# A mixture layer behind attention: 256 instead of 512 plain tokens, Strassen passes of 1,024 tokens, and output weights decoded ahead

## The chip, the cores and the metric

One Trainium2 chip, one core of it. The metric is device time in microseconds (us) of one execution, and lower is better. The engines are TensorE (PE, with its weight loads as PEld), VectorE (DVE), ScalarE (ACT), GpSimd (POOL), and SyncE (SP), which issues most DMAs. Each engine runs its instructions in the order in which they were compiled and waits at the first one that is not ready.

## What is computed

Attention with eight heads of 64 (four local heads, four strided ones), then two feed-forward layers, the second of them gated:

```python
x = attention(q, k, v)                    # 4 x 576 = 2304 tokens, 512 wide
h = x @ w_in                              # 512 -> 2048
x = (h - tanh(h)) @ w_out                 # 2048 -> 512
xn = x / sqrt(mean(x * x) + 1e-6) * rms_g
out = (silu(xn @ w_gate) * (xn @ w_val)) @ w_out2   # 512 -> 1536 -> 512
```

## The kernel before

**Precision.** Every operand of TensorE is kept as a high and a low part, and a product is three matmuls (high by high, low by high, high by low). A block product over 512 inputs is thus a group of 12 matmuls.

**First layer.** The 2,304 tokens go in five groups of 512, 512, 256, 512 and 512 (g = 0 to 4). A group runs 16 units f: `ps_h` (12 matmuls), tanh on ACT, two DVE steps and an ACT cast for the high and low part of `g`, then 12 matmuls into the four banks `ps_x`. Attention of the next group runs beside it, so in the last group there is none, and the SBUF room of attention (on the right side) is free for other pools. At the end of the last group `evac_x` copies the four banks to `xe` on ACT and writes them to DRAM (`x2d`) by DMAs that ACT issues itself.

**Second layer.** `R0` = 512 tokens are worked plainly, in 12 steps f: gate product `ps_h<-xn,w`, value product `ps_m<-xn,w` (12 matmuls each, `pe_gv`), silu and multiplication to `p`, and `pe_o`, which adds 12 matmuls `ps_x<-w,p` into four banks. Gate and value have two banks each, so gate f needs the silu of gate f-2 to be done. The other 1,792 tokens are worked in two Strassen passes j of 2 x `HT` = 2 x 448 tokens, each with six pairs of steps and seven products a pair (`ps_pr`, `ps_q`), 12 matmuls of `HT` columns for each of gate and value. Then `ps_o` adds the output products. The operands of the Strassen passes (`xt1` to `xt6`) are made from `x2` (the normalised rows, `prep_s`) by casts on ACT and DVE and by four subtractions `tr` on POOL (`conv`).

**Weights.** The second layer's 36 weight tiles (gate, val and out2 of 12 steps) arrive packed (`raw`, 512 KB). Decoding one takes ACT `ct` and `ca`, DVE `ct`, ACT `w` (high) and DVE `w` (low). `Stream` `st2` does this in the order of `w2_order`, the first `N1` = 18 of them during the last group, the others during the plain steps. `Store` writes the results to DRAM (`store`, `plain`), from where the Strassen passes fetch them (`wt<-w`). The unpacked tiles lie in a pool `wts` of 22 slots, and raw tiles go into the same pool or into slots that the first layer's weights leave.

**What sets the order.** SP runs in written order from the last group on. PE runs in written order in groups 1 to 3 and in the Strassen passes. Elsewhere a list scheduler of the compiler puts the instructions of an engine in a row. Pools decide the waits: a tile can be written when the last reader of its slot is done, and a `ps_h` or `ps_m` bank when ACT or DVE has read it.

Of the kernel before, what the change touches and what calls it, by code (L numbers as in the profile page):

```python
# [7 lines left out]
F32 = mybir.dt.float32  # L8
# [26 lines left out]
def attn_moe_moe_kernel(  # L35
# [39 lines left out]
    NG = len(groups)  # L75
    R0 = 512
    HT = 448
    NJ = (NT - R0) // (2 * HT)
# [78 lines left out]
    class Weight:  # L157
# [51 lines left out]
    class Stream:  # L209
# [12 lines left out]
        def step(self):  # L222
            i, ws = self.i, self.ws
            self.load_to(min(len(ws), i + 1 + min(self.ahead, max(1, self.slots - 2 - i))))
            if i < len(ws):
                ws[i].bits(self.on_act(i))
            if 0 < i <= len(ws):
# [93 lines left out]
    decode = Decode()  # L321
    xt, tmp = {}, [wts, None, None]

    class Store:
# [12 lines left out]
        def to(self, n):  # L337
            while self.n < min(n, len(w2_order)):
                w = w2[w2_order[self.n]]
                p, i = divmod(w.f, 2)  # L340
                t = w.t.bitcast(F32)
                if w.kind == "out2":
# [10 lines left out]
    store = Store()  # L353

    xh = {}
# [510 lines left out]
    xn = {}  # L866
    HALVES = [(0, 512), (512, 2 * HT)]

    def preps():
        yield from prep_s(0, [(0, R0)], bank_m, pbr)  # L870
        x = xt["raw"]
        t = mid.tile([128, 2, 4, 512], F32R, tag="xs", name="xn")
        for c in range(4):
            nc.scalar.copy(out=t[:, 0, c], in_=x[:, c, :R0])
            nc.vector.tensor_tensor(out=t[:, 1, c], in0=x[:, c, :R0], in1=t[:, 0, c].bitcast(F32), op=ALU.subtract)
# [9 lines left out]
    def pe_gv(j, f):  # L885
        r, n = [], R0
        for kd, pool, tag in (("gate", ps_h, "h"), ("val", ps_m, "m")):
# [26 lines left out]
    def evac_o(j):  # L914
        for t in range(R0 // 128):
# [3 lines left out]
            else:  # L919
                nc.vector.tensor_scalar_mul(out=o, in0=oacc[j][t], scalar1=WS)  # L920

    def prep_s(base, parts, bank, room):
        w = parts[-1][1]
# [5 lines left out]
        for h, (a, e) in enumerate(parts):  # L929
            n = e - a  # L930
            acc, sq = (pbx.tile([128, 512], F32, tag=nm, name=nm)[:, :n] for nm in ("acc", "sq"))
            nc.scalar.activation(out=acc, in_=x[:, 0, a:e], func=ACTF.Square)
# [84 lines left out]
    class Stage:  # L1017
# [45 lines left out]
        def run(self, outs, tick):  # L1063
# [33 lines left out]
            tick(4)  # L1097
            outs(3)

# [38 lines left out]
    wks = [Work(groups[1])]  # L1138
    xq, first_units, pg = [], units[:3], None
    del units[:3]  # L1140
# [59 lines left out]
    def unit(g, f, a, e, pe_work=lambda: None, work=lambda: None):  # L1200
# [7 lines left out]
        g_hi(g, f, a, e)  # L1208
        if g == NG - 1 and f >= 1:
            st2.to(N1 * f // (FA - 1))  # L1210
            store.plain(st2.i - 1)
            store.to(st2.i - 6)
# [17 lines left out]
    for g, f, a, e in units:  # L1230
        if g == 0:
            st1.to(2 * (f + 4))
        elif f == 0:
            if g == 1:
                queue0.close()
                order = ctx.enter_context(ExitStack())
                order.enter_context(tc.manual_schedule(engines={mybir.EngineType.PE}))
            if g == NG - 1:
                order.close()
            assert not wks[-1].pe and not wks[-1].st  # L1240
# [3 lines left out]
        if g == NG - 1 and f == 0:  # L1244
            ctx.enter_context(tc.manual_schedule(engines={mybir.EngineType.SP}))
            poolT.close()
            poolR = ExitStack()
            pbx = ctx.enter_context(tc.tile_pool(name="pbx", bufs=1, side="right", reuse_waits="tile"))
            pbr = poolR.enter_context(tc.tile_pool(name="pbr", bufs=1, side="right", reuse_waits="tile"))
            tmp[0] = poolR.enter_context(tc.tile_pool(name="tmr", bufs=1, side="right", reuse_waits="tile"))  # L1250
# [19 lines left out]

        unit(g, f, a, e, pe_work, work)
        if g == NG - 1:
            if f == 2:
# [32 lines left out]
    store.to(len(w2_order))  # L1306
    pairs[0].fetch((0, 1))
    ctx.enter_context(tc.manual_schedule(engines={mybir.EngineType.PE, mybir.EngineType.SP}))

    def second():  # L1310
        nonlocal pb, osum
        pe_o(0, FB - 1)
        osum = mid.tile([128, 4096], F32, tag="xs", name="osum").rearrange("p (t n) -> p t n", t=8)
        evac_o(0)
# [6 lines left out]
    for j in range(NJ):  # L1321
        for p in range(NP):
# [34 lines left out]
            st.run(outs, tick)  # L1357
            todo += [(st, t) for t in ((4, 5, 6, 3, 0, 1, 2) if end else range(7))]
    for o, t in todo:
# [98 lines left out]
```

## Time and profile before

| | |
|---|---|
| median of 3 runs | 885.1 us (884.06 to 887.2) |
| the profiled execution | 881.58 us, of which 879.8 us is the span |
| PE busy | 866.9 us, 99% of the span |
| DVE, ACT, POOL busy | 619.3, 407.9, 266.3 us |
| chain that ended last | PE 62%, DVE 9%, POOL 7%, issue 2%, ACT 1% |

The profiled execution is 3.5 us below the median. Its stages: groups 0 to 3 end at about 369 us, the last group's output matmuls at 460.75 us, the plain steps at about 557 us, the first Strassen pass at about 707 us, the second at 876 us. A timeline row gives the start, the time from the first start to the last end, the engine, line, operation and tiles, and the number of instructions in the row. Matmuls overlap by a fraction of one, so the pace is read from the start of one row to the start of the next.

### The profile page before, as it was taken

Reading aid. Unit: us, or ns where it says so; the run is one execution under the profiler, and the core shown is the slowest. Engines: PE = TensorE matmul, PEld = TensorE weight load, DVE = VectorE, ACT = ScalarE, POOL = GpSimd, SP = SyncE. Lnnn points to the kernel's source line nnn. Section 1 sums busy time; section 2 is a strip of 40 time slices with the busy share of each in tenths; the row PEclk is TensorE's granted clock in tenths of the full one; section 3 lists DMA queues with packets and bytes.
Section 4 is the critical chain, followed back from the end, with each engine's and each line's share of the span. In section 5 each row is a group of like instructions: output and inputs, shape, how many; then the busy total and the mean of one; then the engine's idle time right before and its main releaser. Section 6 shows DMA issues by size and latency. Waiting matters only on the chain.

```text
span 879.8 us, 14013 instructions
## 1 busy us (share of the span) xinstructions
PE 866.9 (99%) x5091; PEld 739.5 (84%) x5091; DVE 619.3 (70%) x1273; ACT 407.9 (46%) x914; POOL 266.3 (30%) x317
## 2 busy tenths in 40 slices
PE   6999999999999999999999999999999999999998
PEld 4888888888998887888888888988888888888886
DVE  6999788888689887168958981345977953345444
ACT  7987543233544333287838751345332533422320
POOL 0000247694276952000002375395621300000000
PEclk8999999999999999999999999999999999999999
DMA  9964224311313000189928895698666039955002
GB/s 331 385 205 164 86 78 137 112 50 37 117 54 111 27 17 1 37 310 382 383 78 263 276 360 195 236 411 320 239 232 230 19 131 351 390 173 164 1 0 84
DMA packets 62021, 157.83 MB, mean 179 GB/s; under 512 B 9920, under 2 KB 21056, under 8 KB 61952
## 3 DMA queue, kind: packets, MB, share of 16 engines
q1 hardware_dynamic: 60800, 155.89, 49.9%
q10 hardware_dynamic: 1152, 1.05, 0.4%
q8 instruction: 40, 0.66, 0.3%
q14 instruction: 29, 0.24, 0.1%
HBM read 112.87 MB, written 44.04 MB: 178 GB/s over the span
## 4 chain that ended last, share of the span: by engine, by line
PE 62%; DVE 9%; POOL 7%; issue 2%; ACT 1%; DVEq 0%; ACTq 0%; POOLq 0%
PE ps_pr L150 19%; PE ps_o L150 13%; PE ps_x L150 12%; PE ps_h L150 11%; POOL pr L636 5%; DVE so L676 4%; PE ps_m L150 4%; PE ps_q L150 3%; POOL pr L669 1%; DVE tg L821 1%; DVE g L832 1%; DVE sm L412 0%; DVE x L966 0%; DVE sc L641 0%; ACT sm L423 0%
## 5 line engine op out<-in xcount | busy, mean ns | idle before, releaser
L150 PE MATMUL ps_x<-g,w 128*128 128x512 f32 (+1 forms) x984 | 214.7, 366 | 0.0
L150 PE MATMUL ps_h<-xs,w 128*128 128x512 f32 (+1 forms) x984 | 213.7, 365 | 0.6 <-DVE tg L821 0.6
L150 PEld LDWEIGHTS ps_h<-xs,w 128*128 128x128 f32 x984 | 168.9, 189 | 30.7 <-DVE tg L821 1.0
L150 PEld LDWEIGHTS ps_x<-g,w 128*128 128x128 f32 x984 | 168.5, 189 | 30.2 <-ACT g L827 0.2
L150 PE MATMUL ps_pr<-xt,wt 128*128 128x448 f32 x576 | 122.5, 365 | 0.0
L636 POOL TENSOR_TENSOR pr<-sk,sq 128x256 f32<-128x256 f32 (+2 forms) x101 | 82.7, 855 | 130.0 <-DMA sq<-in_q_str_dram 104.2
L150 PE MATMUL ps_o<-wt,p 128*128 128x512 f32 x504 | 120.2, 390 | 0.0
L150 PEld LDWEIGHTS ps_pr<-xt,wt 128*128 128x128 f32 x576 | 107.9, 188 | 10.3 <-DVE s L1040 0.2
L150 PEld LDWEIGHTS ps_o<-wt,p 128*128 128x128 f32 x504 | 94.6, 188 | 18.7
L827 ACT CAST g<-tg 128x512 fp32r<-128x512 f32 (+1 forms) x82 | 46.5, 567 | 102.1 <-DVE tg L821 101.9
L669 POOL TENSOR_TENSOR pr<-sv,se 128x288 f32<-128x288 f32 (+12 forms) x104 | 69.7, 691 | 56.5 <-DVE so L676 19.8
L1059 ACT COPY u<-ps_pr 128x448 f32<-128x448 f32 x72 | 38.2, 533 | 90.4 <-PE ps_pr L150 90.4
L676 DVE TENSOR_REDUCE so<-pr 128x16 f32<-128x272 f32 (+11 forms) x104 | 65.0, 654 | 8.4 <-POOL pr L669 8.0
L821 DVE SCALAR_TENSOR_TENSOR tg<-ps_h,tg 128x512 f32<-128x512 f32 (+1 forms) x82 | 50.8, 620 | 28.0 <-ACT tg L816 27.9
L816 ACT ACTIVATE tg<-ps_h 128x512 f32<-128x512 f32 (+1 forms) x82 | 44.3, 540 | 48.2 <-PE ps_h L150 48.1
L1110 DVE SCALAR_TENSOR_TENSOR osum<-ps_o,osum 128x512 f32<-128x512 f32 x70 | 48.0, 687 | 23.1 <-PE ps_o L150 22.5
L832 DVE TENSOR_TENSOR g<-tg,g 128x512 fp32r<-128x512 f32 (+1 forms) x82 | 55.4, 677 | 12.3 <-ACT g L827 11.7
L980 POOL TENSOR_TENSOR tr<-x 128x896 f32<-128x896 f32 x4 | 10.3, 2575 | 174.0 <-DVE x L966 174.0
L150 PE MATMUL ps_pr<-xt,wo 128*128 128x448 f32 x288 | 60.7, 365 | 0.4 <-ACT u L1059 0.4
L150 PEld LDWEIGHTS ps_pr<-xt,wo 128*128 128x128 f32 x288 | 54.0, 188 | 5.3 <-ACT u L1059 0.8
L188 DVE SCALAR_TENSOR_TENSOR ct<-ca,ct 128x512 uint32<-128x512 uint32 x68 | 51.1, 763 | 6.2 <-ACT ca L178 4.6
L199 DVE TENSOR_TENSOR w<-ct,w 128x512 fp32r<-128x512 f32 x68 | 49.8, 741 | 5.4 <-ACT w L195 5.1
(114 smaller groups left out, 1130.9 us busy)
## 6 DMA issues: line engine op xcount, KB each, us to landing
wt<-w SPq DMA_DIRECT2D x84, 512.0 KB, 6.3
raw<-in_w_out_dram SPq DMA_DIRECT2D x28, 512.0 KB, 7.3
w<-w SPq DMA_DIRECT2D x24, 512.0 KB, 5.9
w<-wo SPq DMA_DIRECT2D x24, 512.0 KB, 7.3
raw<-in_w_in_dram SPq DMA_DIRECT2D x16, 512.0 KB, 9.2
raw<-in_w_gate_dram SPq DMA_DIRECT2D x12, 512.0 KB, 6.4
raw<-in_w_val_dram SPq DMA_DIRECT2D x12, 512.0 KB, 6.7
v<-ct SPq DMA_DIRECT2D x24, 256.0 KB, 5.6
```

What stands on the lines that cost most here:

```text
L150: nc.tensor.matmul(out_, lhsT, rhs, start=start, stop=stop, skip_group_check=True)
L188: nc.vector.scalar_tensor_tensor(out=t, in0=self.a.bitcast(U32), scalar=3, in1=t, op0=ALU.logical_shift_left, op1=ALU.bitwise_or)
L199: eng.tensor_tensor(out=t[:, 1], in0=self.b, in1=t[:, 0].bitcast(F32), op=ALU.subtract)
L636: nc.gpsimd.tensor_tensor(out=pr, in0=self.k[:, a:e, :], in1=self.q[:, c - c0:c - c0 + 1, :].to_broadcast([128, e - a, D]), op=ALU.mult,)
L669: nc.gpsimd.tensor_tensor(out=pr, in0=self.v[:, 0:c + 1, a:e], in1=self.e[:, c - c0, 0:c + 1].unsqueeze(2).to_broadcast([128, c + 1, e - a ...
L676: pend.append(lambda: nc.vector.tensor_reduce(out=o[:, c - g0, a:e], in_=pr.rearrange("l c d -> l d c"), axis=AX.X, op=ALU.add))
L816: nc.scalar.activation(out=t, in_=h_of[g, f, a], func=ACTF.Tanh, scale=WS)
L821: nc.vector.scalar_tensor_tensor(out=t, in0=h_of.pop((g, f, a)), scalar=WS, in1=t, op0=ALU.mult, op1=ALU.subtract)
L827: nc.scalar.copy(out=t[:, 0], in_=t_of[g, f, a])
L832: nc.vector.tensor_tensor(out=t[:, 1], in0=t_of.pop((g, f, a)), in1=t[:, 0].bitcast(F32), op=ALU.subtract)
L1059: nc.scalar.copy(out=u, in_=x[kd])
L1110: nc.vector.scalar_tensor_tensor(out=o, in0=ps, scalar=WS, in1=o, op0=ALU.mult, op1=ALU.add)
```

## The change

- `R0` goes from 512 to 256 and `HT` from 448 to 512. A plain gate or value group is 12 matmuls of 256 columns, `pe_o` has 6 matmuls of 512 columns and two banks, and a Strassen product has 512 columns. Each pass has eight output tiles of 128 tokens in place of seven.
- A class `Early` decodes all 12 out2 tiles in the last two units of group 3 and the first two of group 4, with three raw slots and three work slots in the room that attention leaves, and stores them to DRAM. `load` fetches them back as finished tiles (`w<-w0_7` and so on) when their plain step is near.
- `st2` therefore decodes gate and val alone, from unit 2 of the last group instead of 1, and `N1` is 19.
- In the plain steps raw tiles have three slots of their own (`rawb`) and wait for no slot of `wts`. `wts` has 20 slots instead of 22 (`HELD` 12).
- The first two Strassen tiles (`wt`) are fetched from step 8 on, and not behind all stores.
- SP's written order begins at unit 14 of group 3.

```diff
-    R0 = 512
-    HT = 448
+    R0 = 256
+    HT = 512
...
-    HELD = 10
+    HELD = 12
...
         def load(self):
             kind, f = self.kind, self.f
-            pool, tag = room_of(w1_at.get((kind, f), 0))
+            if kind == "out2" and f < NE:
+                p, i = divmod(f, 2)
+                self.t = wts.tile([128, 2, 4, 128], F32R, tag="w", name="w")
+                nc.sync.dma_start(out=self.t.bitcast(F32).rearrange("p s c f -> p (s c f)"), in_=pairs[p].store[7 + i])
+                return
+            self.fetch(*(tmp[3] or room_of(w1_at.get((kind, f), 0))))
...
-    N1 = 18
+    N1 = 19
+    NE = 12
...
+    class Early:
...
+        def run(self):
+            ws, n = self.ws, NE
+            for k in range(min(3, n)):
+                ws[k].fetch(self.pool, "r")
+            yield
+            for k in range(n + 2):
+                if k < n:
+                    ws[k].bits(True)
+                    if k + 3 < n:
+                        ws[k + 3].fetch(self.pool, "r")
+                if 1 <= k <= n:
+                    ws[k - 1].split(self.pool, "e", nc.vector)
+                if k >= 2:
+                    p, i = divmod(ws[k - 2].f, 2)
+                    nc.sync.dma_start(
+                        out=pairs[p].store[7 + i], in_=ws[k - 2].t.bitcast(F32).rearrange("p s c f -> p (s c f)")
+                    )
+                yield
...
+        if g == NG - 2 and f == 14:
...
+            ctx.enter_context(tc.manual_schedule(engines={mybir.EngineType.SP}))
...
+            early = Early(soon).run()
...
+    tmp[3] = (poolB.enter_context(tc.tile_pool(name="rawb", bufs=3, reuse_waits="tile")), "raw")
...
     for f in range(FB):
+        if f == FB - 4:
+            pairs[0].fetch((0, 1))
...
-    pairs[0].fetch((0, 1))
```

Three places where instructions stand in another order. First ACT at the end of the last group and the start of the plain steps: `xe` is the copy of a `ps_x` bank, `acc<-ps_r` the first step behind the matmuls of the norm, `xt` an operand for the Strassen passes, `ct`, `ca` and `w` are decoding, and `s` is silu. Before, from the first `xe`:

```order
L852 ACTIVATE xe_5551<-ps_x_4833 128x512
L852 ACTIVATE xe_5555<-ps_x_4834 128x512
L858 DMA x2d_100<-xe_5551 128x256 x2
L858 DMA x2d_100<-xe_5555 128x256 x2
L852 ACTIVATE xe_5559<-ps_x_4835 128x512
L896 ACT_TABLE_LOAD
L896 ACTIVATE s_5617<-ps_h_5604 128x512
L999 CAST xt1_5577<-x2_5114 128x896
```

Of the changed kernel, from the last `xe`. Ahead of these rows stand three `xe`, five of the DMA issues, one `w` cast and the sixth DMA issue:

```order
L890 ACTIVATE xe_5669<-ps_x_4971 128x512
L995 ACTIVATE acc_5530<-ps_r_5642,cole_59 128x512
L1043 CAST xt1_5683<-x2_5238 128x1024
L1043 CAST xt2_5684<-x2_5238 128x1024
L896 DMA x2d_100<-xe_5669 128x256 x2
L203 CAST w_5703<-ct_5606 128x512
L184 ACTIVATE ct_5751<-raw_5597,colf_58 128x512
L186 ACTIVATE ca_5753<-raw_5597 128x512
L184 ACTIVATE ct_5758<-raw_5604,colf_58 128x512
L186 ACTIVATE ca_5760<-raw_5604 128x512
L934 ACT_TABLE_LOAD
L934 ACTIVATE s_5720<-ps_h_5707 128x256
```

The first silu stood behind three `xe`, four DMA issues and the table load, and now stands behind all of the `xe`, all eight DMA issues, the norm's `acc`, both `xt` casts, two `w` casts and the scaling of two raw tiles.

PE at the same place. Before, from the last bank of the last group:

```order
L150 MATMUL ps_x_4836<-g_5486,w_1637 128x512 x3
L150 MATMUL ps_m_5619<-xn_5062,w_4828 128x512 x12
L150 MATMUL ps_h_5669<-xn_5062,w_4932 128x512 x8
L150 MATMUL ps_m_5684<-xn_5062,w_4984 128x512 x12
L150 MATMUL ps_h_5731<-xn_5062,w_5044 128x512 x12
L150 MATMUL ps_m_5746<-xn_5062,w_5094 128x512 x12
```

Of the changed kernel (`ps_h_5707`, gate step 0, has been worked earlier, as `ps_h_5604` before):

```order
L150 MATMUL ps_x_4971<-g_5595,w_1637 128x512 x3
L150 MATMUL ps_m_5722<-xn_5180,w_5016 128x256 x5
L150 MATMUL ps_r_5642<-s2_5576,ones_4923 128x512
L150 MATMUL ps_m_5722<-xn_5180,w_5016 128x256 x3
L150 MATMUL ps_r_5642<-s2_5576,ones_4923 128x512
L150 MATMUL ps_m_5722<-xn_5180,w_5016 128x256 x4
L150 MATMUL ps_h_5769<-xn_5180,w_5070 128x256
L150 MATMUL ps_m_5784<-xn_5180,w_5117 128x256 x12
L150 MATMUL ps_h_5821<-xn_5180,w_5212 128x256 x12
```

The norm's `ps_r` moved from ahead of the last bank into the first value group, and holds a bank of `ps_m` there. `ps_m_5784` takes the bank that `ps_r_5642` leaves when `acc_5530` has read it, and `ps_h_5821` takes the bank that `s_5720` reads.

PE at the end of the plain steps. Before, from the last gate group:

```order
L150 MATMUL ps_h_6316<-xn_5062,w_6153 128x512 x12
L150 MATMUL ps_m_6331<-xn_5062,w_6208 128x512 x12
L150 MATMUL ps_x_5773<-w_6007,p_6246 128x512 x3
L150 MATMUL ps_x_5774<-w_6007,p_6246 128x512 x3
L150 MATMUL ps_x_5775<-w_6007,p_6246 128x512 x3
L150 MATMUL ps_x_5776<-w_6007,p_6246 128x512 x3
```

Of the changed kernel, from the end of output step 10 on:

```order
L150 MATMUL ps_x_5864<-w_6091,p_6292 128x512 x2
L150 MATMUL ps_pr_6356<-xt1_5683,wt_6153 128x512 x6
L150 MATMUL ps_pr_6363<-xt1_5683,wt_6155 128x512 x6
L150 MATMUL ps_m_6322<-xn_5180,w_6215 128x256 x12
L150 MATMUL ps_x_5863<-w_6164,p_6336 128x512 x3
L150 MATMUL ps_x_5864<-w_6164,p_6336 128x512 x3
```

The last value group stood ahead of two output steps and of the first Strassen product, and now stands behind all of these, with its own output step straight behind it.

## Rows read from the trace of the kernel before

**Rows 1.** The page: busy time and share of each engine.

```profile
PE 866.9 (99%) x5091; PEld 739.5 (84%) x5091; DVE 619.3 (70%) x1273; ACT 407.9 (46%) x914; POOL 266.3 (30%) x317
```

**Rows 2.** PE's waits, 340 to 880 us: total, times, longest in us.

```profile
PE ps_pr L150 <- ACT u L1059: 0.4, 1, 0.4
```

**Rows 3.** PE timeline: start, us, operation, tiles, count; 256 and 448 columns.

```profile
232.02 1.60 PE L150 MATMUL ps_x<-g,w 128*128 128x256 f32 x12
233.46 1.60 PE L150 MATMUL ps_h<-xs,w 128*128 128x256 f32 x12
...
706.70 2.59 PE L150 MATMUL ps_pr<-xt,wt 128*128 128x448 f32 x12
709.13 2.59 PE L150 MATMUL ps_q<-xt,wt 128*128 128x448 f32 x12
```

**Rows 4.** PE timeline at the start of the plain steps.

```profile
460.75 2.88 PE L150 MATMUL ps_m<-xn,w 128*128 128x512 f32 x12
...
465.28 2.88 PE L150 MATMUL ps_m<-xn,w 128*128 128x512 f32 x12
468.00 2.88 PE L150 MATMUL ps_h<-xn,w 128*128 128x512 f32 x12
```

**Rows 5.** ACT timeline at the same place (ACTq: issues of DMAs).

```profile
458.90 1.28 ACT L852 ACTIVATE xe<-ps_x 128x512 f32<-128x512 f32 x2
459.65 1.82 ACTq L858 DMA_DIRECT2D x2d<-xe  x4
461.51 0.60 ACT L852 ACTIVATE xe<-ps_x 128x512 f32<-128x512 f32 x1 [1.33 <-DMA x2d<-xe]
462.13 1.28 ACT L896 ACT_TABLE_LOAD   x1
463.42 0.60 ACT L896 ACTIVATE s<-ps_h 128x512 f32<-128x512 f32 x1
...
463.91 0.93 ACT L999 CAST xt<-x 128x896 fp32r<-128x896 f32 x1
...
468.28 0.76 ACT L176 ACTIVATE ct<-raw,colf 128x512 uint32<-128x512 uint16 x1 [0.94 <-DMA x2d<-xe]
468.95 0.66 ACT L178 ACTIVATE ca<-raw 128x512 f32<-128x512 f32 x1
```

**Rows 6.** Costliest groups by form: the 256-column tanh, multiply and cast of group 2.

```profile
L821 DVE SCALAR_TENSOR_TENSOR tg<-ps_h,tg 128x256 f32<-128x256 f32 x20 | 8.4, 418 | 3.1 <-ACT tg L816 3.1
L827 ACT CAST g<-tg 128x256 fp32r<-128x256 f32 x20 | 8.1, 406 | 13.2 <-DVE tg L821 13.2
L816 ACT ACTIVATE tg<-ps_h 128x256 f32<-128x256 f32 x20 | 7.6, 381 | 10.5 <-PE ps_h L150 10.5
```

**Rows 7.** Windows of 2 us at the start: busy of each engine, granted clock, DMA share, GB/s.

```profile
8.00:10.00 2.00, 0.00 (x0) 0.00 (x0) 1.61 (x7) 1.37 (x9) 0.00 (x0) 1.00 1.02 398
...
14.00:16.00 2.00, 2.00 (x34) 1.71 (x32) 1.86 (x9) 2.00 (x10) 0.00 (x0) 0.50 0.98 266
...
18.00:20.00 2.00, 1.33 (x68) 1.02 (x67) 1.86 (x9) 1.75 (x10) 0.00 (x0) 0.98 0.99 395
```

**Rows 8.** PE, DVE and ACT timelines at the last value group and output steps.

```profile
546.88 5.60 PE L150 MATMUL ps_x<-w,p 128*128 128x512 f32 x24
547.15 0.69 DVE L897 SCALAR_TENSOR_TENSOR s<-ps_m,s 128x512 f32<-128x512 f32 x1 [6.09 <-PE ps_m L150]
547.87 0.62 ACT L899 CAST p<-s 128x512 fp32r<-128x512 f32 x1 [2.86 <-DVE s L897]
```

**Rows 9.** POOL and DVE timelines while POOL makes the Strassen operands.

```profile
481.53 2.35 POOL L980 TENSOR_TENSOR tr<-x,tr 128x896 f32<-128x896 f32 x1 [0.65 <-DVE x L966]
481.82 2.61 DVE L188 SCALAR_TENSOR_TENSOR ct<-ca,ct 128x512 uint32<-128x512 uint32 x1
```

**Rows 10.** The page: DMA issues, KB each, median us to landing.

```profile
wt<-w SPq DMA_DIRECT2D x84, 512.0 KB, 6.3
```

**Rows 11.** The window from group 3's end to the first units of group 4.

```profile
340.00:390.00 50.00, 50.00 (x248) 41.26 (x248) 19.74 (x35) 23.28 (x43) 0.00 (x0) 1.00 0.35 117
```

More of the change, by code (lines that the diff above doesn't have):

```diff
@@ L162, in load, with fetch @@
             kind, f = self.kind, self.f
-            pool, tag = room_of(w1_at.get((kind, f), 0))
+            if kind == "out2" and f < NE:
[4 more added lines that the diff above has]
+            self.fetch(*(tmp[3] or room_of(w1_at.get((kind, f), 0))))
+        def fetch(self, pool, tag):
+            kind, f = self.kind, self.f
             r = pool.tile([128, 4, 128], w_in.dtype, tag=tag, name="raw")
@@ L224, in step @@
             self.load_to(min(len(ws), i + 1 + min(self.ahead, max(1, self.slots - 2 - i))))
-            if i < len(ws):
+            if i < len(ws) and not (ws[i].kind == "out2" and ws[i].f < NE):
                 ws[i].bits(self.on_act(i))
-            if 0 < i <= len(ws):
+            if 0 < i <= len(ws) and not (ws[i - 1].kind == "out2" and ws[i - 1].f < NE):
                 pool, tag, eng = self.place(i - 1)
@@ L341, in to @@
                 t = w.t.bitcast(F32)
+                if w.kind == "out2" and w.f < NE:
+                    self.n += 1
+                    continue
                 if w.kind == "out2":
@@ L353, in attn_moe_moe_kernel, with __init__ @@
     store = Store()
+    class Early:
+        def __init__(self, pool):
+            self.pool = pool
+            self.ws = [w2["out2", f] for f in range(NE)]
+        def run(self):
[16 more added lines that the diff above has]
+                yield
     xh = {}
@@ L866, in attn_moe_moe_kernel @@
     xn = {}
[L867 removed]
+    HALVES = [(0, HT), (HT, 2 * HT)]
     def preps():
@@ L930, in prep_s @@
             n = e - a
-            acc, sq = (pbx.tile([128, 512], F32, tag=nm, name=nm)[:, :n] for nm in ("acc", "sq"))
+            if pbs:
+                acc, sq = (pbs.tile([128, 512], F32, tag=nm, name=nm)[:, :n] for nm in ("acc", "sq"))
+            else:
+                t = wts.tile([128, 2, 512], F32, tag="w", name="acc")
+                acc, sq = t[:, 0, :n], t[:, 1, :n]
             nc.scalar.activation(out=acc, in_=x[:, 0, a:e], func=ACTF.Square)
@@ L1097, in run @@
             tick(4)
-            outs(3)
+            outs(3 if HT < 512 else 4)
         def out(self, t):
@@ L1138, in attn_moe_moe_kernel @@
     wks = [Work(groups[1])]
-    xq, first_units, pg = [], units[:3], None
+    xq, first_units, pg, early = [], units[:3], None, None
     del units[:3]
@@ L1208, in unit @@
         g_hi(g, f, a, e)
-        if g == NG - 1 and f >= 1:
-            st2.to(N1 * f // (FA - 1))
+        if g == NG - 1 and f >= 2:
+            st2.to(N1 * (f - 1) // (FA - 2))
             store.plain(st2.i - 1)
@@ L1239, in attn_moe_moe_kernel @@
                 order.close()
-            assert not wks[-1].pe and not wks[-1].st
+            if g < NG - 1:
+                assert not wks[-1].pe and not wks[-1].st
             new_x(g + 1)
@@ L1243, in attn_moe_moe_kernel @@
                 wks.append(Work(groups[g + 1], EARLY if g == 1 else ()))
-        if g == NG - 1 and f == 0:
+        if g == NG - 2 and f == 14:
+            assert not wks[-1].pe and not wks[-1].st
+            order.close()
             ctx.enter_context(tc.manual_schedule(engines={mybir.EngineType.SP}))
+            order = ctx.enter_context(ExitStack())
+            order.enter_context(tc.manual_schedule(engines={mybir.EngineType.PE}))
             poolT.close()
+            poolE = ExitStack()
+            soon = poolE.enter_context(tc.tile_pool(name="soon", bufs=3, side="right", reuse_waits="tile"))
+            tmp[2] = poolE.enter_context(tc.tile_pool(name="ct2", bufs=2, side="right", reuse_waits="tile"))
+            early = Early(soon).run()
+        if g == NG - 1 and f == 2:
+            for _ in early:
+                pass
+            poolE.close()
             poolR = ExitStack()
             pbx = ctx.enter_context(tc.tile_pool(name="pbx", bufs=1, side="right", reuse_waits="tile"))
+            poolS = ExitStack()
+            pbs = poolS.enter_context(tc.tile_pool(name="pbs", bufs=1, side="right", reuse_waits="tile"))
             pbr = poolR.enter_context(tc.tile_pool(name="pbr", bufs=1, side="right", reuse_waits="tile"))
@@ L1271, in attn_moe_moe_kernel @@
         unit(g, f, a, e, pe_work, work)
+        if early is not None and (g < NG - 1 or f < 2):
+            for _ in range(4):
+                next(early, None)
         if g == NG - 1:
@@ L1357, in attn_moe_moe_kernel @@
             st.run(outs, tick)
-            todo += [(st, t) for t in ((4, 5, 6, 3, 0, 1, 2) if end else range(7))]
+            todo += [(st, t) for t in ((4, 5, 6, 7, 3, 0, 1, 2) if end else range(8))]
     for o, t in todo:
```

17 lines of the change are left out of this document (10 added, 7 removed).

## The prediction

> **What bounds the kernel now.** I read the page's busy shares first: PE is busy 866.9 of the 879.8 us of the span, DVE and ACT far less [rows 1]. Then PE's waits: from 340 us to the end there is one, of 0.4 us [rows 2]. So nearly every microsecond from the last groups on is matmul time. Two things can change the end: how many columns PE streams at which pace, and whether the new order puts a wait in front of PE where there was none. Other engines count only where PE reads what they make or needs a bank that they empty. The timelines at the two ends of the plain steps show how much room PE has there [rows 4, 5, 8]. The sum is made against the profiled execution (881.58 us, 3.5 below the median of 885.1), and its difference is then put on the median, since both kernels are timed in ordinary runs.
>
> **Matmuls.** A row's pace is the distance to the next start. Twelve matmuls of 512 columns take 468.00 - 465.28 = 2.72 us [rows 4], 12 of 448 take 709.13 - 706.70 = 2.43, and 12 of 256 take 233.46 - 232.02 = 1.44 [rows 3]. The plain steps have 24 gate and value groups, which become shorter by 2.72 - 1.44 = 1.28 us: -30.7. The Strassen passes have 2 x 6 x 7 products of 12 matmuls, each longer by 0.29: +24.4. Output matmuls move from plain to Strassen, 648 of 512 columns before and after: nothing. The norm's columns follow the tokens: nothing. PE term **-6.3 us**. The 0.29 is a small difference of two rows, and 0.03 more in it would be +2.5, so I keep -6.3 to -3.8.
>
> The Trainium skill (TensorE: Matmul & The Clock Gate, section "Wait — 56ns, not 53.3ns?") speaks against the change here: it gives a warm matmul as its columns at 2.4 GHz plus about 2.5 ns, by which 64 more columns cost 26.7 ns. The rows show 226.7 - 202.5 = 24.2 ns. By the page the PE term would be -30.7 + 26.9 = -3.8 us, an estimate; by the rows it is -6.3.
>
> **The start of the plain steps.** E is the end of the last group's last output matmul, 460.75 us before [rows 4]. Before, silu of gate 0 ran from 463.42 to 464.02, E + 3.3 [rows 5], and gate 2, which needs its bank, started at 468.00 without a wait [rows 4]. Now this silu stands far back in ACT's row. I add up ACT's row with the durations of [rows 5]. A successor starts about 0.1 us before its forerunner ends (463.42 + 0.60 against 463.91), so an operation of 0.60 costs 0.5. The third `xe` can start when its bank is done, about E - 0.2. From E - 0.1 on five DMA issues at 1.82 / 4 = 0.455 take until E + 2.2. The `w` cast waits for the first value group, whose 12 matmuls of 256 columns and two of the norm (1.44 + 0.45) end at E + 1.9, so it runs to about E + 2.7, and a sixth issue beside it. The last `xe` (which also waits for the first copies to reach DRAM, 1.33 us before [rows 5]) and the `acc` behind it end at about **E + 3.9**. PE wants to start `ps_m_5784` at E + 2.0 and needs the bank that `acc` reads: a wait of **1.9 us**. Then come two `xt` casts, 0.93 at 896 columns, so about 0.96 each at 1,024 after the overlap (E + 5.8); a `w` cast (E + 6.3); `ct`, `ca` twice at 0.67 and 0.56 (E + 8.8); the table load, 1.28 (E + 10.0); and silu at 256 columns, 0.38 by the tanh of that width [rows 6]: **E + 10.4**. `ps_m_5784` is through by E + 5.4 at the pace of [rows 3], and `ps_h_5821` needs the bank that this silu reads: a wait of **5.0 us**. Everything behind it on PE is queued. Together **+6.9 us**. The row has 12 to 14 instructions with durations known to a tenth, so I keep +5.5 to +8.5. That nothing hides it is seen from [rows 2]: PE had no idle time here before that the wait could use up.
>
> **PE's clock.** In the trace of before the only comparable idle stretch is near the start: PE does nothing from 8 to 10 us, and then all three windows from 12 to 18 us show a granted clock of 0.50, the lower level of 1.2 GHz, until it is back at 0.98 in 18 to 20 [rows 7]. Six us at half clock are 3.0 us of lost work. In the changed kernel PE works 1.5 of the 8.4 us from E + 2.0 to E + 10.4, so I expect the fall. How much of the low stretch lies beside work and not inside the wait is not shown. Bounds 0 and +3.0; nearer to the row than to nothing, so **+2.0**.
>
> **The end of the plain steps.** Before, the last value group ended at about 546.9, multiplication began at 547.15 and the high cast of `p` ended at 548.49, while PE worked 24 matmuls of older steps [rows 8]. Now `ps_x<-w,p_6336` follows its value group directly. The chain at 256 columns is 0.27 to the start of the DVE step, 0.42, and 0.41 for the cast [rows 6, 8]: **+1.2 us**, between 0.9 and 1.7 (the low part).
>
> The first Strassen product moves ahead of that value group, and its tiles `wt` are fetched earlier. On SP this fetch stands behind the store of a decoded value tile whose ACT work is behind `xt4`, which waits for POOL's fourth `tr`. By the same kind of addition POOL is done at E + 37 to 41, the store is issued at E + 42 to 46, and the tiles land at E + 48 to 53 with 6.3 us a load [rows 10]. PE reaches the product at E + 45.8 by pace alone, and at E + 52.7 or later with the waits above. So the early waits pay for this one: 0 to +2, taken as **+0.6**. The spread of POOL is contention: a DVE decode step of 0.68 us took 2.61 beside a `tr` of 2.35 [rows 9], and `tr` grows by 1024/896. The same stretching could delay a `p` of steps 3 to 5 by up to 4 us without the first wait; behind it this is hidden.
>
> **The last group and the room of attention.** Twelve decodes of three ACT and two DVE steps (about 1.75 and 1.2 us each, 21 and 14 in all, by the paces above) move to 342 to 392 us, where DVE was busy 19.7 and ACT 23.3 of 50 us [rows 11], and out of the plain steps. Both fit, ACT with little to spare. They delay the first loads of gate and value tiles, which stand behind `Early`'s last store on SP. Decode, norm and `xn` then still come some us ahead of PE by my addition, with the tightest places at the last output steps of group 3 and steps 3 and 10 of group 4: 0 to +2, **+0.6**. The Strassen stages give ACT and DVE 512 columns in place of 448 on engines with half their time free: nothing.
>
> **Sum.** -6.3 + 6.9 + 2.0 + 1.2 + 0.6 + 0.6 = **+5.0 us**: 886.6 on the profiled scale, **890.1** on the median's.
>
> **Rivals.**
> (a) Both waits at the start, but the clock stays: for it speaks that the wait is broken by a group of 1.5 us, against it [rows 7]. Without the 2.0 it is +3.0, **888.1**.
> (b) The waits at the start don't arise, and the change is **faster**. The price is ACT's row between the last group's copies and the first silu. It decides from E + 5.4: a silu done by then lets PE through, and then only the end and the last group cost, -6.3 + 1.2 + 0.6 + 0.6 = -3.9, **881.2**. For it speaks that ACT is busy under half of the span [rows 1]; against it, that the row is fixed and ACT cannot take the silu first.
> (c) More is lost in decoding than I count: the moved decodes don't lighten the plain steps, because the loads for gate and value come late and SP's stores hold the Strassen tiles back. It decides where the `wt` tiles land after E + 55. With 2 us in the last group and 4 at the end instead of 1.2 in all, it is +9.8, **894.9**. For it: [rows 9]; against it: the time that the first wait gives.
> (d) By the page's pace for matmuls, everything else as forecast, it is +7.5, **892.6**; [rows 3, 4] speak against it.
>
> **Chances.** Forecast 0.42, (a) 0.20, (b) 0.13, (c) 0.15, (d) 0.10. A measurement of this kernel can tell about 0.3%, 2.65 us, from no change. Case (b) is faster, with some of it within the bound: 0.12. Of (a) about half, and of the forecast a tenth or so where the waits are at their short end, are within: 0.2. The rest is slower: 0.68. The range holds (a), the forecast, (d) and most of (c), and at its low end the forecast with the shortest waits and no fall of the clock (-6.3 + 5.5 + 0.9 = +0.1), and a little of (b): 883.5 to 896.0.
>
> **What would show it.** In the profile of the changed kernel: 12 Strassen matmuls at 2.72 a row; a wait of PE on ACT `acc` of about 1.9 us and one on ACT `s` of about 5 us right behind the last group; ACT's table load some 9 us after E; a granted clock below 1 in the slices behind; a gap of about 1.2 us ahead of the last plain output step. The prediction is wrong if PE waits less than 3 us there, if the product pace is not 2.72, or if PE waits several us in group 4 or at the `wt` tiles.

## The result and the profile after

| | before | after |
|---|---|---|
| median of 6 runs each | 885.37 us (884.06 to 887.81) | 892.89 us (891.12 to 895.17) |
| ratio after : before | | 1.008, 95% interval 1.0059 to 1.0101 |
| the profiled execution, and its span | 881.58, 879.8 | 893.28, 891.5 |

The change makes the kernel 0.8% slower, 7.5 us by the medians. The two profiled executions lie 11.7 us apart in span. Some 2.2 us of that have come up by 26 us, in code that is the same in both (the `ps_v` matmuls that start at 24.07 us before start at 26.29 after), so about 9.5 us are to be explained in these two executions.

The busy shares, which answer to [rows 1]:

```profile
PE 866.0 (97%) x5091; PEld 723.4 (81%) x5091; DVE 633.5 (71%) x1282; ACT 413.3 (46%) x915; POOL 271.0 (30%) x317
```

PE is busy for 0.9 us less, but its share fell from 99% to 97%. PE's waits from 335 us to the end (total, times, longest, in us), which answer to [rows 2]:

```profile
PE ps_h L150 <- ACT s L934: 4.8, 1, 4.8
PE ps_x L150 <- DVE p L938: 2.3, 1, 2.3
PE ps_m L150 <- ACT acc L995: 1.7, 1, 1.7
PE ps_x L150 <- ACT p L937: 1.0, 1, 1.0
PE ps_h L150 <- DVE tg L859: 0.7, 1, 0.7
PE ps_pr L150 <- DVE s L1084: 0.5, 1, 0.5
PE ps_pr L150 <- DVE v L1096: 0.5, 1, 0.5
PE ps_pr L150 <- DVE s L1093: 0.5, 1, 0.5
PE ps_x L150 <- ACT g L865: 0.2, 1, 0.2
```

One wait of 0.4 us has become nine of 12.2 us in all. The one on DVE `tg`, which ends at 335.72 us, is not new: before, it took 0.61 us and ended at 333.50, ahead of the stretch of [rows 2]. PE's timeline at the start of the plain steps, which answers to [rows 4]; E is now 461.84 us:

```profile
463.73 0.28 PE L150 MATMUL ps_h<-xn,w 128*128 128x256 f32 x1
465.67 1.69 PE L150 MATMUL ps_m<-xn,w 128*128 128x256 f32 x12 [1.67 <-ACT acc L995]
472.20 4.98 PE L150 MATMUL ps_h<-xn,w 128*128 128x256 f32 x24 [4.84 <-ACT s L934]
477.02 1.24 PE L150 MATMUL ps_m<-xn,w 128*128 128x256 f32 x9
```

ACT's timeline there, which answers to [rows 5]:

```profile
464.94 0.68 ACT L995 ACTIVATE acc<-ps_r,cole 128x512 f32<-128x512 f32 x1
...
465.51 1.05 ACT L1043 CAST xt<-x 128x1024 fp32r<-128x1024 f32 x1
...
470.47 1.28 ACT L934 ACT_TABLE_LOAD   x1
471.77 0.66 ACT L934 ACTIVATE s<-ps_h 128x256 f32<-128x256 f32 x2
```

`acc` ends at 465.62, E + 3.8. The first silu starts 1.30 us behind the start of the table load and ends at about 472.15, E + 10.3. Both PE waits end where ACT's row says.

Windows of the same stretch (length, busy of PE, PEld, DVE, ACT, POOL with counts, granted clock, DMA share, GB/s):

```profile
470.00:473.00 3.00, 0.80 (x3) 0.80 (x4) 2.91 (x6) 2.97 (x6) 0.00 (x0) 0.50 0.63 179
473.00:480.00 7.00, 7.00 (x42) 6.74 (x42) 6.09 (x13) 4.74 (x10) 0.00 (x0) 0.76 0.94 294
480.00:490.00 10.00, 10.00 (x74) 9.48 (x74) 9.75 (x10) 5.94 (x11) 6.39 (x3) 1.00 0.89 355
490.00:500.00 10.00, 7.67 (x40) 6.77 (x39) 10.00 (x13) 6.15 (x12) 4.03 (x2) 0.83 0.66 186
```

The clock is at its lower level of 1.2 GHz after the long wait, and falls a second time after 490 us. In both places DVE is busy nearly all the time. The second place in the timelines of POOL, DVE and PE, which answers to [rows 9]:

```profile
486.40 2.43 POOL L1024 TENSOR_TENSOR tr<-x,tr 128x1024 f32<-128x1024 f32 x1 [0.77 <-PE ps_m L150]
488.76 2.86 POOL L1024 TENSOR_TENSOR tr<-x 128x1024 f32<-128x1024 f32 x1
...
486.77 2.60 DVE L196 SCALAR_TENSOR_TENSOR ct<-ca,ct 128x512 uint32<-128x512 uint32 x1
489.30 3.41 DVE L1044 TENSOR_TENSOR xt<-x,xt 128x1024 fp32r<-128x1024 f32 x1
...
492.97 0.41 DVE L938 TENSOR_TENSOR p<-s,p 128x256 fp32r<-128x256 f32 x1
493.30 0.68 DVE L196 SCALAR_TENSOR_TENSOR ct<-ca,ct 128x512 uint32<-128x512 uint32 x1
493.90 1.21 DVE L1044 TENSOR_TENSOR xt<-tr,xt 128x1024 fp32r<-128x1024 f32 x1
...
493.43 1.20 PE L150 MATMUL ps_x<-w,p 128*128 128x512 f32 x2 [2.33 <-DVE p L938]
494.43 2.34 PE L150 MATMUL ps_h<-xn,w 128*128 128x256 f32 x10
```

`ct` and `xt` take 0.68 and 1.21 us when POOL is idle (the last two DVE rows). Here each ends 0.54 and 1.09 us after the POOL subtraction that it started beside (489.37 against 488.83, and 492.71 against 491.62), so each spends nearly all of POOL's time waiting. `p`, which PE needs, is queued behind both.

Last, the end of the plain steps, which answers to [rows 3, 8]:

```profile
526.01 1.67 PE L150 MATMUL ps_x<-w,p 128*128 128x512 f32 x6 [0.95 <-ACT p L937]
527.52 2.90 PE L150 MATMUL ps_pr<-xt,wo 128*128 128x512 f32 x12
530.26 2.88 PE L150 MATMUL ps_q<-xt,wt 128*128 128x512 f32 x12
```

### The profile page after: what moved, and what is told of

Same layout as the page of the kernel before. It is cut to its first block, busy times and chain, and to the rows that moved or that the text cites. A ratio compares the mean times of both kernels' runs of the same rounds, so it can differ in the third digit from the quotient of the medians.

```text
span 891.5 us, 14064 instructions
## 1 busy us (share of the span) xinstructions
PE 866.0 (97%) x5091; PEld 723.4 (81%) x5091; DVE 633.5 (71%) x1282; ACT 413.3 (46%) x915; POOL 271.0 (30%) x317
## 4 chain that ended last, share of the span: by engine, by line
PE 58%; DVE 10%; POOL 7%; issue 2%; ACT 2%; DMA 2%; SPq 0%; DVEq 0%; ACTq 0%; POOLq 0%
PE ps_pr L150 20%; PE ps_o L150 14%; PE ps_x L150 9%; PE ps_h L150 9%; POOL pr L674 5%; DVE so L714 4%; PE ps_q L150 4%; PE ps_m L150 1%; POOL pr L707 1%; DVE tg L859 1%; DVE g L870 1%; DMA w<-w 1%; DMA wt<-w 1%; POOL ws L302 0%; DVE sm L450 0%
## 5 line engine op out<-in xcount | busy, mean ns | idle before, releaser
L150 PE MATMUL ps_pr<-xt,wt 128*128 128x512 f32 x576 | 137.4, 390 | 1.5 <-DVE s L1084 0.5
L150 PE MATMUL ps_o<-wt,p 128*128 128x512 f32 x576 | 135.9, 389 | 0.0
L150 PEld LDWEIGHTS ps_o<-wt,p 128*128 128x128 f32 x576 | 108.1, 188 | 22.5
L1103 ACT COPY u<-ps_pr 128x512 f32<-128x512 f32 x72 | 41.9, 587 | 102.4 <-PE ps_pr L150 102.4
L1154 DVE SCALAR_TENSOR_TENSOR osum<-ps_o,osum 128x512 f32<-128x512 f32 x80 | 54.6, 687 | 26.5 <-PE ps_o L150 26.2
L150 PE MATMUL ps_pr<-xt,wo 128*128 128x512 f32 x288 | 67.4, 389 | 0.0
L1024 POOL TENSOR_TENSOR tr<-x 128x1024 f32<-128x1024 f32 x4 | 11.8, 2948 | 176.1 <-DMA raw<-in_w_val_dram 140.8
L870 DVE TENSOR_TENSOR g<-tg,g 128x512 fp32r<-128x512 f32 (+1 forms) x82 | 54.9, 671 | 10.4 <-ACT g L865 9.8
L196 DVE SCALAR_TENSOR_TENSOR ct<-ca,ct 128x512 uint32<-128x512 uint32 x68 | 49.1, 731 | 18.6 <-ACT ca L186 18.1
```

The costliest lines, as they stand in the source:

```text
L150: nc.tensor.matmul(out_, lhsT, rhs, start=start, stop=stop, skip_group_check=True)
L196: nc.vector.scalar_tensor_tensor(out=t, in0=self.a.bitcast(U32), scalar=3, in1=t, op0=ALU.logical_shift_left, op1=ALU.bitwise_or)
L870: nc.vector.tensor_tensor(out=t[:, 1], in0=t_of.pop((g, f, a)), in1=t[:, 0].bitcast(F32), op=ALU.subtract)
L1103: nc.scalar.copy(out=u, in_=x[kd])
L1154: nc.vector.scalar_tensor_tensor(out=o, in0=ps, scalar=WS, in1=o, op0=ALU.mult, op1=ALU.add)
```

## The experiments

Each is a change of the kernel after, or of the experiment that is named. Ratios are to the kernel before, timed beside it on the same chip; since the experiments ran on several chips, ratios compare them better than medians do. "Stretch" is the time from E to the first `ps_pr<-xt,wo`: 65.68 us in the profile after, 96.73 before.

### The order at the start

The pool `pb` of the silu results was opened behind `rawb` and, so I held, lay over room of `xe`. **e1_pb_first** opens it first:

```diff
+    pb = poolB.enter_context(tc.tile_pool(name="pb", bufs=2, reuse_waits="tile"))
     tmp[3] = (poolB.enter_context(tc.tile_pool(name="rawb", bufs=3, reuse_waits="tile")), "raw")
-    pb = poolB.enter_context(tc.tile_pool(name="pb", bufs=2, reuse_waits="tile"))
```

> The changed kernel with two pools in another order: pb (silu and p tiles) is opened ahead of rawb. Theory: silu stands late on ACT only because pb, behind rawb, lies over the room of the xe tiles, whose copies to DRAM must be done first. With pb ahead, the first silu follows the last xe directly and ends at about E + 4.9 (E: end of the last group's output matmuls). PE then waits about 2.9 us instead of 6.9 right behind E, and the clock falls less: 885.5 to 888.5 us, against 892.9 of the changed kernel. Rival (the decode work behind is the limit): PE's wait moves to the p tiles or weights of the later steps, and the time stays above 891.

**e2_pb_first_sp_copies** is e1 with the `x2d` copies of the last group issued by SP:

```diff
-        queue = nc.sync if g < NG - 1 else nc.scalar
+        queue = nc.sync
```

> As the one with pb ahead, and the eight copies of xe to DRAM are issued by SP in place of ACT. Theory: the first silu ends at about E + 2.2, PE waits under 0.5 us there and its clock stays at full speed: 8 to 9 us less than the changed kernel if nothing is given back, 884 to 885; the matmul term alone would be 885.4 - 6.5 = 878.9, and the wait at the p tiles beside POOL's subtractions (2.5 and 1.6 of the clock), the last plain output step (1.1) and the first Strassen pair (1.5) lie on top. Rival: with PE some 7 us earlier the p tiles and Strassen weight tiles come too late by as much, 888 to 892.

e1 took 894.52 us, ratio 1.0118 (1.0084 to 1.0152). Silu came straight behind the last `xe` and the table load, the wait for it was 2.8 us, and none on `acc` was left. e2 took 892.51, ratio 1.0087 (1.0061 to 1.0114), with no wait at the start of the plain steps and the clock at 1.00 there. PE's waits of e2, the largest:

```profile
PE ps_x L150 <- DVE p L938: 3.6, 2, 2.1
PE ps_x L150 <- ACT p L937: 2.1, 3, 1.0
PE ps_pr L150 <- DVE s L1093: 1.2, 2, 0.7
PE ps_m L150 <- ACT w L203: 1.1, 1, 1.1
```

So the order of two pools is what put silu behind the copies, and the wait for it can be removed. But the time stays: the 6.5 us of waits are replaced by others further on, and the clock falls at 505 us instead (0.69 in 505 to 510). The stretch is 63.36 us, 2.3 shorter than after, in a total time that the intervals can't tell from that of the kernel after. What sets the end of the plain steps lies behind PE's first waits.

**e3_filled_wait** puts 40 matmuls of 256 columns, whose result nobody reads, into the first wait, to hold the clock.

```diff
+        if f == 1:
+            fill = bank_x("ps_f")
+            for i in range(40):
+                mm(fill[:, :256], ones, xn[0][:, 0, 0], i == 0, i == 39)
```

> The changed kernel with 40 matmuls of 256 columns (4.8 us, result unused) between gate step 1 and value step 1, where PE waits 6.9 us; silu of step 0 stands one cast later, about 0.5 us. Theory: the wait as a whole stays (2 to 2.6 us of it empty), but the granted clock stays at 1.00 from 463 to 480 us, and the 1.9 us that PE lost at half clock behind the wait come back: 890.5 to 892. Rival (the fall of the clock costs nothing, since the work behind waits for other engines anyway): 893 to 894.

895.8 us, ratio 1.0121 (1.0095 to 1.0147). The clock held at 1.00 from 463 to 470 us, but 3.0 us of the wait for silu were left behind the added matmuls, the clock fell then (0.83 in 470 to 480), and a new wait of 3.0 us on DVE `s` came. It is inconclusive on the clock's price.

### What holds the plain steps

**e4_no_pool** leaves out the four POOL subtractions of the first pass (the operands are made from one summand):

```diff
+            if len(plainly) < 4:
+                plainly.append(name)
+                xt[name] = p
+                return p
```

> The changed kernel with the four subtractions of POOL for the first Strassen pass left out (the casts read one operand as it is); one more cast stands ahead of the first silu, about 1 us. Theory: the wait of 2.3 us of PE for the low part of p of step 3 comes from DVE steps stretched beside POOL, so it vanishes, with the second fall of the clock (1.6 us): 889 to 891. Rival (DVE has too much of its own to do there): the wait stays above 1.5 us and the time is 893 to 894.5.

**e5_no_pool_pb_first** does so on top of e2.

> pb ahead of rawb, copies issued by SP, and the four subtractions of POOL for the first Strassen pass left out (the casts read one operand as it is). Theory: with the wait behind E gone, the plain steps take what DVE needs beside POOL (DVE is busy 10 of 10 us from 480 to 510 in both kernels with pb first, and its steps are stretched); without POOL the stretch from E to the first product with wo falls from 63.4 us to 52.5 to 55 (matmuls alone 51.4), and the time to 881.5 to 885. Rival (DVE's own steps or the loads are the limit): the stretch stays above 59 us, 888 or more.

e4 took 891.29 us, ratio 1.0068 (1.0043 to 1.0094): the waits on `p` are gone, those on silu (5.8, as one more cast stands ahead of it) and `acc` (1.7) remain, and the stretch is 61.62. e5 took **884.75**, ratio 1.0005 (0.9993 to 1.0018), some 7 us below e2 (0.0082 of the ratio), from which it differs only by the subtractions. Its stretch is 56.86. The ratios are 1.0080 after, 1.0087 with silu first (e2), 1.0068 without the subtractions (e4), and 1.0005 with both. Neither cure alone moves it by more than the intervals, both together move it by 0.0075, some 6.6 us. The profiled executions show that a single cure is given back only in part: the stretch is 2.3 us shorter with silu first, 4.1 without the subtractions and 8.8 with both. In e4 little of this is seen in the time, because E itself lies 2.6 us later (464.39 against 461.84); 1.3 us of that have come up by the `ps_v` matmuls of the start (27.57 against 26.29), in code that is the same.

Is it that DVE waits for POOL's results, that POOL slows DVE, or that DVE has too much to do? **e11_sub_unread** is e2 with the subtractions made on POOL as before, but not read (the casts read the first summand):

```diff
+            plainly.append(name)
-            return out
+            return p if len(plainly) <= 4 else out
```

> pb ahead of rawb, copies issued by SP; POOL still makes the four subtractions for the first Strassen pass, but nobody reads them (the casts read one operand as it is), which leaves their use out of the result. It tells apart the two ways in which POOL holds the plain steps. If DVE steps are stretched beside POOL: as with the subtractions read, 890 to 893, with DVE's means above 0.8 us for the 512-column steps. If ACT and DVE wait in order for POOL's results: as without POOL, 884 to 887. I expect the larger part from the waiting in order, since POOL's four run one behind another behind the norm: 885 to 889.

**e12_low_parts_act** is e2 with the low parts of the seven operands `xt` of the first pass written by ACT, as copies, in place of a subtraction on DVE:

```diff
+        if len(plainly) <= 7:
+            nc.scalar.copy(out=t[:, 1], in_=v)
+        else:
+            nc.vector.tensor_tensor(out=t[:, 1], in0=v, in1=t[:, 0].bitcast(F32), op=ALU.subtract)
-        nc.vector.tensor_tensor(out=t[:, 1], in0=v, in1=t[:, 0].bitcast(F32), op=ALU.subtract)
```

> pb ahead of rawb, copies issued by SP; the low parts of the seven operands of the first Strassen pass are written by ACT as plain copies in place of DVE's subtraction (their value is left out), so DVE has some 10 us less to do between E and the Strassen passes, and POOL works as before. If DVE's time is what is short, the stretch from E to the first product with wo falls from 63.4 to below 59 us and the time to 886 to 889. If POOL's chain is what is waited for, the stretch stays above 61 us and the time at 890.5 to 893.

**e10_silu_first_sub_dve** is e2 with the four subtractions made by DVE itself:

```diff
-            nc.gpsimd.tensor_tensor(out=out, in0=p, in1=q, op=ALU.subtract)
+            eng = nc.gpsimd if len(plainly) >= 4 else nc.vector
+            plainly.append(name)
+            eng.tensor_tensor(out=out, in0=p, in1=q, op=ALU.subtract)
```

> The changed kernel with pb ahead of rawb, the copies of xe issued by SP, and the four subtractions for the first Strassen pass on DVE in place of POOL. Theory (DVE steps stretched beside POOL bound the plain steps): DVE gains 8 us and pays 4.6, so the stretch from E to the first product with wo falls from 63.4 to 57 to 60 us: 885 to 889 against 892.5 with POOL. Rival (DVE short of time whatever POOL does): 891 or more.

e11 took 894.72 us, ratio 1.0103 (1.0088 to 1.0118); e12 891.68, ratio 1.0061 (1.0039 to 1.0083); e10 889.14, ratio 1.0052 (1.0035 to 1.0069). Three of the costliest DVE groups between 462 and 530 us, of e11 (line, operation, count, then busy us, mean ns, idle before):

```profile
L1047 DVE TENSOR_TENSOR xt<-x,xt 128x1024 fp32r<-128x1024 f32 x7 | 10.4, 1526 | 0.0
L196 DVE SCALAR_TENSOR_TENSOR ct<-ca,ct 128x512 uint32<-128x512 uint32 x10 | 9.5, 962 | 4.6 <-ACT ca L186 4.6
...
L1010 DVE SCALAR_TENSOR_TENSOR x<-x,gcol,sq 128x512 f32<-128x512 f32 x4 | 4.9, 1282 | 0.0
```

and of e5, where POOL makes none of them:

```profile
L1050 DVE TENSOR_TENSOR xt<-x,xt 128x1024 fp32r<-128x1024 f32 x7 | 8.3, 1226 | 0.0
L196 DVE SCALAR_TENSOR_TENSOR ct<-ca,ct 128x512 uint32<-128x512 uint32 x10 | 7.7, 782 | 2.9 <-ACT ca L186 2.9
...
L1010 DVE SCALAR_TENSOR_TENSOR x<-x,gcol,sq 128x512 f32<-128x512 f32 x4 | 2.7, 750 | 0.0
```

In e11 nobody waits for POOL's results, and yet the same steps are about as long as in the kernel after (`ct` 922 ns, `x` 1282), and the kernel is no faster than e2. So it is the running of the subtractions beside DVE that costs, not the dependence on them; my own expectation of a gain here failed. e12 takes about 11 us of work off DVE (the two `xt` groups of e2 in this stretch) and gains 0.8 us by the medians and 2.3 by the ratios, with intervals that overlap: DVE's total does not look like the main limit, though ACT has the copies to make in its place, and what that costs was not separated. What counts is that single DVE steps are held for 2 to 3 us, and `p` with them (waits of 3.5 us in e11, 3.1 in e12). In e11 it is `p` itself, 0.41 us long elsewhere, that is held beside a subtraction which nobody reads, and PE waits for it:

```profile
493.50 2.79 POOL L1026 TENSOR_TENSOR tr<-x 128x1024 f32<-128x1024 f32 x1
494.01 2.57 DVE L938 TENSOR_TENSOR p<-s,p 128x256 fp32r<-128x256 f32 x1
496.63 1.22 PE L150 MATMUL ps_x<-w,p 128*128 128x512 f32 x2 [3.48 <-DVE p L938]
```

In e10 DVE makes three of the subtractions in 1.22 us each and the fourth in 1.76. The kernel is some 3 us below e2 (0.0035 of the ratio), with intervals that overlap, so this gain is not certain; the waits on DVE `p` fall from 3.6 to 0.7 us in all, and those on ACT `p` grow from 2.1 to 4.2.

The Trainium skill (SBUF — State Buffer, section "🔬 SBUF: two separate sides") says that GpSimd shares a pair of ports with VectorE as an exclusive lock: when a VectorE step has two inputs in SBUF and a GpSimd operation reads SBUF, the one that starts second is blocked until the first is done. The rows agree: the DVE steps `ct` and `xt` in the profile after end 0.54 and 1.09 us after POOL's, about their own lengths of 0.68 and 1.21.

### Preparing earlier

**e6_norm_ahead** is e2 with the preparation of the norm and the operands done in fewer units of the last group, and **e7_norm_ahead_sub_dve** is e6 with the subtractions on DVE, as in e10:

```diff
-            for _ in range(0 if pg is None else 3 if f < 8 else 2):
+            for _ in range(0 if pg is None else 3 if f < 13 else 2):
```

> pb ahead of rawb, copies issued by SP, and the norm of the second half of x2 (8 chain steps and 4 products on DVE, 8 to 10 us of it) done before E: three steps of it a unit up to unit 12 of the last group. Theory (DVE bounds the plain steps): the waits at p fall by about half, 886 to 889.5 against 892.5 with the norm where it was. Rival (POOL's subtractions alone, wherever they lie, or a wait given back in the last group): 891 or more.

> As the one with the norm ahead, and the four subtractions for the first pass run on DVE (4 x about 1.15 us) in place of POOL (4 x 2.7 us or more, beside which DVE steps were stretched by some 8 us in all). Theory: DVE's stretched steps cost more than its own four, so 1.5 to 4 us less than with POOL: 883 to 887. Rival (DVE is short of time, not of the port): as slow or slower than with POOL.

e6 took 896.53 us, ratio 1.0125 (1.0108 to 1.0142): the wait on DVE `p` is 1.9 us, but a value weight now comes 4.6 us late (PE on ACT `w`), and the clock falls behind it. e7 took 889.91, ratio 1.0072 (1.0043 to 1.0102), with 2.9 us on that `w`. So less is waited for `p`, but the weight comes late: neither run is faster than the one that it was made from, and e6 has 0.0038 more in its ratio than e2.

### The sizes undone

**e8_sizes_undone** keeps the whole change but the sizes (and, with them, seven output tiles a pass). **e9_sizes_undone_silu_first** opens `pb` first of all in addition and lets SP issue the copies.

```diff
-    R0 = 256
-    HT = 512
+    R0 = 512
+    HT = 448
```

> The changed kernel with the old sizes, 512 plain tokens and passes of 896; out2 tiles ahead, raw slots, 20 slots and the early fetch stay. Theory: silu of step 0 stands as late as in the changed kernel, about E + 9.5, but a value group of 512 columns lies ahead of the bank that waits for it, so PE waits 4 to 5 us there and loses 1 to 2 to its clock; the rest of the plain steps has 96.7 us of matmuls for about 55 us of DVE work and shows no wait: 888.5 to 891. Rival (the smaller plain steps are the whole cause): no wait above 1 us behind E, 884 to 886.

> The old sizes (512 plain tokens, passes of 896) with the rest of the change, the pool pb opened ahead of tmp, and the copies of xe issued by SP, so that the first silu follows the third xe on ACT. Theory: everything that the rest of the change costs at the old sizes (9.5 us in the run with the sizes undone) is the late silu and the clock behind it, so the waits behind E vanish and the time comes back to 884 to 886. Rival (out2 tiles ahead, the 20 slots or the fetches cost something of their own): 887 to 892, with waits elsewhere.

e8 took 893.96 us, ratio 1.0100 (1.0085 to 1.0115). All of PE's waits of e8 from 335 us on:

```profile
PE ps_h L150 <- ACT s L934: 5.0, 1, 5.0
PE ps_m L150 <- ACT acc L995: 1.4, 1, 1.4
PE ps_h L150 <- DVE tg L859: 0.7, 1, 0.7
```

PE's timeline behind the longest:

```profile
478.55 7.83 PE L150 MATMUL ps_h<-xn,w 128*128 128x512 f32 x21 [5.05 <-ACT s L934]
```

The 21 matmuls take 7.83 us, against 21/12 x 2.72 = 4.8 at the pace of [rows 4]. So the rest of the change costs some 9.5 us without the new sizes, nearly all of it at the start of the plain steps: waits of 6.4 us and about 2.9 of clock. There is no wait on `p`, although POOL makes its subtractions: with 512 plain tokens PE has twice the work between them. e9 took 888.14, ratio 1.0032 (1.0015 to 1.0049): with silu first, this part of the change costs 0.3%, and the new sizes then add to the loss (e2's 1.0087 against 1.0032), although they save 6.3 us of matmuls.

No version with the new sizes beat the kernel before: e5, which leaves the subtractions out, is level with it, and e10 comes next with 889.14 us. Of the times that I expected by my theories only e5's held. The others came out above their ranges, e4 and e10 by less than 0.4 us; e1, e6 and e9 came out by the rival that is named with them, and e12, where two theories were left open, by the second.

## Why the prediction was right, and where it was not

I forecast 890.1 us, slower, between 883.5 and 896.0; it is 892.89. On the medians that is 2.8 us off. Between the two profiled executions it is more: +5.0 was forecast against 9.5, and a range 12.5 us wide covers both. The terms against the profile, in us:

| term | forecast | measured | from |
|---|---|---|---|
| matmuls | -6.3 | about -6.3 | remainder of the stages without waits and clock, below |
| waits at the start | +6.9 | +6.9 | idle 1.67 and 4.84; start to start 0.4 more |
| clock | +2.0 | +3.4 | 24 matmuls in 4.82 for 2.88 us; 12 in 3.13 for 1.65 behind the second fall |
| last output step | +1.2 | +1.1 | the wait at 526.01 |
| `wt` tiles | +0.6 | 0 | no wait at the first product |
| last group | +0.6 | about +0.6 | E is 1.1 later, 2.2 of which is the start, where gate 0 (-1.28) and `ps_r` (-0.46) alone would give -1.7 |
| `p` of the early steps | 0, "hidden" | +2.5 | the wait at 493.43 |
| Strassen passes | 0 | +1.5 | three waits of 0.5; before, one of 0.4 |
| sum | +5.0 | +9.7 | 9.5 to be explained; 0.2 less behind the last matmul |

**Matmuls: right.** From E to the end the profile after is 10.85 us longer (65.68 + 360.35 - 96.73 - 318.45, the latter of each pair from the first `ps_pr<-xt,wo` to the end of the last matmul). Less 15.4 us of waits and clock (6.9 + 3.4 + 1.1 + 2.5 + 1.5) that is -4.6; gate 0, worked ahead of E, is shorter by 1.28, and the norm's `ps_r` moved behind E with 0.46: -6.3. As this is a remainder, the sum of the table does not test it, and it is known to half a us or so. The test is the pace: a product now takes 530.26 - 527.52 = 2.74 us, and the next 2.72. By the page of the Trainium skill that I weighed (TensorE: Matmul & The Clock Gate, "Wait — 56ns, not 53.3ns?") it would have been -3.8; the trace stands by the rows of before.

**Waits at the start: right in place, size and cause.** Adding up ACT's row gave `acc` at E + 3.9 and silu at E + 10.4; they came at E + 3.8 and E + 10.3. I had not seen why silu was there; e1 shows that it is the place of its pool.

**Clock: the fall was foreseen, the term mis-sized.** I counted one fall of 2.0 us. The first cost 1.9; the second, behind a wait that I took to be hidden, cost 1.5 more.

**The failed step: "behind it this is hidden".** I knew that a DVE step beside POOL is stretched [rows 9] and bounded the delay of `p` with up to 4 us, but held that the first waits of PE would cover it. They do not: behind 6.9 us of waits PE still lost 2.5 us to `p`, and without the wait for silu and `acc` (e2) the waits on DVE `p` are 3.6 in place of 2.3, so the first waits hid some 1.3 us of it. The reason is argued and not tested by itself: `p` needs PE's own products, so a late PE delays `s` and `p` as well, and in PE's waits DVE does not run dry (busy 2.91 of 3.00 us from 470 to 473). Before, the same stretching cost nothing: the stretch was 96.7 us with DVE busy in 63.1 of it, now it is 65.7 with 50.5, and e8, which has the old sizes again, shows no wait on `p`.

**The Strassen stages, put at "nothing", cost about 1.5 us** in three short waits on DVE `s` and `v`, two of them at the first pair. They were not tested.

**The `wt` tiles, put at +0.6, cost nothing**: no wait at the first product.

**The rivals.** (a), the same waits with the clock unmoved, is refuted by the granted clock of 0.50 and 0.76 in the windows from 470 to 480 us. (b) held that without the first waits the kernel would reach 881.2. e2 has no such waits at the start of the plain steps and takes 892.51, so (b)'s price was wrong, and with it the reading of my own sum: 6.9 + 2.0 us is about what PE lost there, but not what the kernel owes to it. Only with POOL's subtractions gone too (e5) do 8 us come back, and even then it ends level with before, since 3.0 us of waits on ACT `p` and a fall of the clock remain. (c), more lost in decoding, came close in time (894.9), but not by its mechanism: the tiles `wt` were in time. (d) came nearest of all (892.6), by luck: a product takes 2.72 us, as the rows of before have it, and what lies above the forecast are the waits on `p` and in the Strassen passes and the second fall of the clock, none of which (d) has. What of e5's remaining time goes to the decoding ahead in the last group was not measured by itself.

## What to carry to other kernels

When a stage is cut short, check what ran hidden in it: here the same decoding and the same POOL work that cost nothing beside 97 us of matmuls held PE in 66. A wait that a sum prices correctly is worth its price only if nothing else is late by nearly as much behind it; take both away in one run before you believe either price. A tile's place in SBUF is part of the order, since it decides whose release an instruction waits for, and so where a scheduler puts it.

## What the runs showed of the hardware

**DVE beside POOL.** A POOL subtraction of 2.4 to 2.9 us held DVE steps with two SBUF operands until it ended: the 512-column `ct` went from 0.68 to 2.6 us, and the 256-column `p` from 0.41 to 2.57 in e11, where nobody reads what POOL makes. In the kernel after, the step `s<-ps_m,s` that starts at 486.44 us, with one operand in PSUM, took its 0.41 us beside the subtraction that had started at 486.40.

**The clock after short waits.** PE's waits of about 2 to 3 us were sometimes followed by a stretch at the lower level and sometimes not. Rows of e5, e10 and e12, and behind the first a window of e5:

```profile
477.76 2.08 PE L150 MATMUL ps_x<-w,p 128*128 128x512 f32 x4 [2.04 <-ACT p L937]
...
478.00:480.00 2.00, 2.00 (x6) 1.61 (x7) 2.00 (x5) 1.40 (x3) 0.00 (x0) 0.50 0.99 331
```

```profile
506.47 3.46 PE L150 MATMUL ps_x<-w,p 128*128 128x512 f32 x12 [2.04 <-ACT p L937]
```

```profile
487.93 0.73 PE L150 MATMUL ps_x<-w,p 128*128 128x512 f32 x2 [3.10 <-DVE p L938]
```

In e5 four matmuls then take 2.08 us, at 0.50, and some 1.6 us are lost by the time that the next 12 are through (4 in 1.88 us from start to start for 0.91, 12 in 2.10 for 1.44). In e10, behind a wait of the same 2.04, the windows from 504 to 512 us show 1.00; in e12 those from 478 to 492 show it too, even with the 3.10. Waits of up to 1.5 us (e1, e2) showed no fall. So a wait of 2.04 us cost its length in e10 and 3.7 us in e5, and one run does not tell which it will be.
